# Row maxima of a fused attention and MLP layer, turned by VectorE's 32x32 transposition instead of by products

## The chip, the cores and the metric

One core of a Trainium2 chip runs the whole program. The metric is the device time of one execution in microseconds (us), as the median of several executions. The engines are named as the profile names them: PE is TensorE's matmul unit and PEld its weight load, DVE is VectorE, ACT is ScalarE, POOL is GpSimd, SP is SyncE, which here issues every DMA. SBUF is the on-chip working memory, PSUM the accumulators, in eight banks of 128 partitions by 512 float32.

## The reference

The input is `x` of 2048 rows by 512 columns, float32. The layer adds three things: the input itself, an attention block, and an MLP with tanh-GELU, both of these on the normalised rows:

```python
xn = _layernorm(x, axis=-1)
return x + _A_ref(xn, A_wqkv, A_wo) + _B_ref(xn, B_w1, B_b1, B_w2, B_b2)

# _A_ref: 32 heads of 16 columns
scores = jnp.einsum("bhqd,bhkd->bhqk", q, k) * (Dh ** -0.5)
p = _softmax(scores, axis=-1)
o = jnp.einsum("bhqk,bhkd->bhqd", p, v)

# _B_ref: 512 -> 1792 -> 512
h = _gelu(jnp.einsum("bsd,df->bsf", x, w1) + b1)
return jnp.einsum("bsf,fd->bsd", h, w2) + b2
```

The softmax subtracts each row's maximum over all 2048 keys before the exponential, so every head needs the maximum of each of its 2048 score rows first.

## The kernel before, in words

Operands of the products are split into a high and a low float16 part, so that float16 products give nearly float32 results.

**Attention** goes through the scores twice. In the *S pass* PE computes a 128 query x 512 key tile of scores into a PSUM bank `pS`, and DVE reduces it to a column of maxima (line 259, `mt<-pS`). In the *E pass* PE computes the transposed scores (keys on partitions, queries on columns) into a bank `pT`, with the negated maximum added by two more rows of the contraction, and ACT takes the exponential (line 304, `pe<-pT`). PE then multiplies by the values (`pV`). The maxima therefore have to come from the S pass, where they are a column per query tile, into rows of the operand `qst` (rows 62, 63, 126 and 127), where the E pass reads them.

The work is cut into 32 **blocks** (8 groups of four heads x 4 blocks of 512 queries), a block into 16 **units**, and a unit into two **half-units**. A unit holds four S tiles and four E tiles of the block that lies 20 units behind (`LEAD = 20`). In each half-unit PE does two S and two E tiles, then value products of an earlier unit together with a number of **dense** products (`pD`): projections, the MLP and so on, taken from a stream of `Group`s.

The order of the instructions on each engine is written out by the program itself: `unit` emits the tiles, `tick` at the end of each unit runs what `later(n, fn)` has put off by n units, and `pooled` hands work to POOL in portions. Nothing reorders the result.

**The end of a block (the place of the change).** `s_end` (line 262) runs after the last unit of a block's S pass. DVE reduces the 64 collected columns to 16 columns of negated maxima, one per head and query tile, in `mneg`, 128 x 32 with the last 16 columns zero (line 270). `store` is put off by one unit. In it, a bank `pt` is taken out of the same rotation of three banks from which the S tiles take theirs (`banks("S")`); two products with the identity (line 277), each over 64 partitions, turn `mneg` into 2 x 32 rows of 64; DVE writes these as a high and a low float16 part (`mhl`, lines 280 and 281); SP stores both to the DRAM tensor `m_d` in two transfers (line 284) and then loads them into the rows of `qst` in four (line 289), the first two for one pair of heads, the next two for the other.

Since the S tiles use three banks in turn, a tile can start on PE when the reduction of the tile three turns before has ended on DVE; the bank `pt` counts as a turn.

**The tanh of the GELU** is an ACT instruction (line 983) that `gelu` puts into the stream when POOL has prepared its input. Before, it was put off once, by a unit, when at most 8 products were left on the two sides of the current dense group, or no group was open.

Of the kernel before, what the change touches and what calls it, by code (L numbers as in the profile page):

```python
# [8 lines left out]
F32 = mybir.dt.float32  # L9
# [8 lines left out]
P = 128  # L18
# [30 lines left out]
def layer_kernel(ctx: ExitStack, tc: tile.TileContext, x, wqkv, wo, w1, b1, w2, b2, out):  # L49
# [163 lines left out]
    def later(n, fn, local=False):  # L213
        queue.append((slot[0] + n, fn, local))
# [47 lines left out]
    def s_end(u):  # L262

        t, i = divmod(u, 16)
        if i < 15:
            return
        g, qb = divmod(t, NQB)
        qs = qst[g % 2]
        mneg = mnegs[t % 2]
        nc.vector.tensor_reduce(mneg[:, :16], mt_of[t].rearrange("p h t k -> p (h t) k"), axis=AX.X, op=ALU.max, negate=True)  # L270
        given("dve", 220)

        def store():

            pt = banks("S")
            for a in range(2):
                nc.tensor.matmul(pt[32 * a:32 * a + 32, :64], mneg[64 * a:64 * a + 64, :],
                                 ident[64 * a:64 * a + 64, 64 * a:64 * a + 64], start=True, stop=True)
            mhl = work.tile([64, 2, 64], F16, name="mhl", bufs=2)
            nc.vector.tensor_scalar_mul(mhl[:, 0], pt[:64, :64], 1.0 / MROW)  # L280
            nc.vector.scalar_tensor_tensor(mhl[:, 1], pt[:64, :64], 1.0 / MROW, mhl[:, 0], op0=ALU.mult, op1=ALU.subtract)
            given("dve", 300)
            for a in range(2):
                nc.sync.dma_start(m_d[t, :, :, 64 * a:64 * a + 64], mhl[32 * a:32 * a + 16])
            for p in range(2):
                for a in range(2):
                    h = 2 * p + a
                    dst = qs[p][qb][64 * a + 62:64 * a + 64, :].rearrange("r (t q) -> r t q", q=P)
                    nc.sync.dma_start(dst, m_d[t, 4 * h:4 * h + 4].rearrange("t r q -> r t q"))

        later(1, store)
# [678 lines left out]
    def mlp():  # L970
# [5 lines left out]
        def gelu(hh, g, b, f):  # L976
            t1 = m2.tile([P, QB], F32, name="t1", bufs=2)

            def tanh(again=1):
                if again and (cur[0] is None or cur[0].left(0) + cur[0].left(1) <= 8):  # L980
                    later(1, lambda: tanh(0), True)
                    return
                nc.scalar.activation(t1, t1, AF.Tanh, scale=GELU_C * GELU_A)
                given("act", 600)
                later(1, rest, True)
# [217 lines left out]
```

## Time and profile before

| | us |
|---|---|
| median of 3 runs (1508.39 to 1509.23) | 1509.2 |
| the profiled execution | 1510.58 |
| its span, first to last instruction | 1508.8 |
| PE busy | 1474.4 |
| DVE busy | 1378.3 |
| ACT busy | 1233.8 |
| POOL busy | 716.5 |
| mean granted TensorE clock, as a share | 0.993 |

The busy time of PE is modelled and counts products that run side by side in quarters of the array once; DVE's instructions overlap their neighbours by some tens of nanoseconds. So neither number says alone which engine is waited for: that is read from the order of starts around a place. In the timeline view a line is a run of instructions of one kind on one engine: its start, its length from first start to last end, the engine, the source line, the operation, what is written and read, the shapes, and how many. Idle time of the engine just before stands in brackets with what ended it.

The kernel's first 130 us (normalisation, first projections) and its last 90 us (no S tiles any more) are stages of their own. Between them blocks follow each other some 41 us apart: `mneg` starts at 1168.14 and at 1209.25 us, for instance.

### The profile page before, as it was taken

The page shows a single profiled execution, that of the slowest core. Times are in us where ns is not written, and L with a number is a line of the kernel's source. Part 1 is how long each engine was busy: PE and PEld are TensorE (multiplying, and loading weights), DVE is VectorE, ACT ScalarE, POOL GpSimd, SP SyncE. Part 2 cuts the span into 40 slices and gives each one's busy share as a digit, 9 for nine tenths or more (in the row PEclk, how much of TensorE's full clock was granted, in tenths as well). Part 3 has the DMA queues.
Part 4 walks back from the last instruction along what each step waited for, and adds up shares of the span by engine and source line. Part 5 has one row for each costly group of instructions (what it writes and reads, how often), then busy time and mean ns, then how long its engine had stood idle before and what let it go on. Part 6 is the DMA issues. An engine that isn't in the chain of part 4 may idle for free.

```text
span 1508.8 us, 87920 instructions
## 1 busy us (share of the span) xinstructions
PE 1474.4 (98%) x39971; PEld 908.1 (60%) x39971; DVE 1378.3 (91%) x2372; ACT 1233.8 (82%) x2326; POOL 716.5 (47%) x750
## 2 busy tenths in 40 slices
PE   8998999999999999999999999999999999999997
PEld 4434556656666666666666666666666666666563
DVE  7898999999999999999999999999999999999612
ACT  5315878899999889999898998998999999988771
POOL 4113598547665545537544554665264465511000
PEclk9999999999999999999999999999999999999998
DMA  6454576633211311121112211121112111022412
GB/s 201 133 172 128 169 217 220 207 102 95 71 37 44 89 42 37 36 78 44 36 50 63 59 36 37 35 83 57 37 42 63 51 33 33 23 68 76 155 37 88
DMA packets 113677, 123.82 MB, mean 82 GB/s; under 512 B 24988, under 2 KB 85276, under 8 KB 113304
## 3 DMA queue, kind: packets, MB, share of 16 engines
q1 hardware_dynamic: 113304, 118.21, 25.6%
q8 instruction: 312, 5.11, 1.4%
q14 instruction: 61, 0.50, 0.1%
HBM read 80.61 MB, written 37.34 MB: 78 GB/s over the span
## 4 chain that ended last, share of the span: by engine, by line
PE 81%; DVE 15%; issue 2%; DMA 1%; ACT 0%; POOL 0%; SPq 0%; ACTq 0%; POOLq 0%
PE pV L170 21%; PE pD L170 20%; PE pS L170 19%; PE pT L170 15%; DVE mt L259 13%; PE pT L441 1%; PE pS L441 1%; DVE amx L675 1%; PE pT L540 1%; PE pD L441 1%; PE pV L540 0%; DVE mneg L270 0%; DMA wch<-in_B_w_dram 0%; DMA xs<-in_A_x_dram 0%; DVE bs L709 0%
## 5 line engine op out<-in xcount | busy, mean ns | idle before, releaser
L259 DVE TENSOR_REDUCE mt<-pS 128x1 f32<-128x512 f32 x2048 | 1278.7, 682 | 40.5 <-PE pS L170 23.5
L304 ACT ACTIVATE pe<-pT 128x512 f32<-128x512 f32 x2048 | 1099.6, 601 | 144.8 <-PE pS L170 62.3
L170 PE MATMUL pV<-pe,vv 64*32 64x512 f32 x8192 | 1088.8, 598 | 1.5 <-issue 1.5
L170 PE MATMUL pT<-qst,kst 64*32 64x512 f16 x8192 | 669.7, 377 | 3.3 <-DMA qst<-m_d 1.4
L170 PE MATMUL pS<-kst,qst 62*32 62x512 f16 x8192 | 637.9, 378 | 9.6 <-DVE mt L259 6.2
L170 PE MATMUL pD<-xb,wc 64*32 64x512 f16 x5376 | 371.8, 375 | 0.0
L170 PE MATMUL pD<-w_s,g 64*32 64x512 f16 (+1 forms) x6144 | 361.8, 348 | 0.0
L170 PEld LDWEIGHTS <-kst 64*32 64x32 f16 x8192 | 254.0, 92 | 129.1 <-issue 49.7
L170 PEld LDWEIGHTS <-qst 62*32 62x32 f16 x8192 | 246.9, 92 | 138.6 <-issue 64.1
L170 PEld LDWEIGHTS <-g 64*32 64x32 f16 x6144 | 195.3, 92 | 84.6 <-issue 0.8
L170 PEld LDWEIGHTS <-wc 64*32 64x32 f16 x5376 | 177.4, 92 | 95.5
L170 PEld LDWEIGHTS pV<-pe,vv 64*32 64x32 f32 x8192 | 176.9, 105 | 5.5 <-issue 2.2
L1018 POOL TENSOR_SCALAR hh<-hh,fac,b_s 128x512 f32<-128x512 f32 x56 | 43.0, 768 | 271.5 <-ACT hh L1016 271.5
L170 PE MATMUL pD<-xt,wqk_h 64*32 64x512 f16 x1920 | 128.6, 375 | 3.1 <-issue 3.1
L360 POOL TENSOR_TENSOR osb<-osb,rb 128x512 f32<-128x512 f32 x31 | 39.8, 1283 | 138.4 <-DMA rb<-den_d 130.2
L1045 POOL TENSOR_TENSOR xa<-xa,yt 128x512 f32<-128x512 f32 x32 | 41.0, 1281 | 111.2 <-ACT yt L1043 111.2
L170 PEld LDWEIGHTS <-wqk_h 64*32 64x32 f16 x1920 | 59.5, 92 | 32.5 <-issue 5.8
L1082 DVE SCALAR_TENSOR_TENSOR ac<-pS,gs,ac 128x512 f32<-128x512 f32 x20 | 15.0, 751 | 65.2 <-PE pS L170 55.5
L996 POOL TENSOR_TENSOR t<-t,hh 128x512 f32<-128x512 f32 x56 | 71.8, 1282 | 4.7
L989 POOL TENSOR_TENSOR t<-t,hh 128x512 f32<-128x512 f32 x56 | 71.8, 1282 | 4.7
L991 POOL TENSOR_TENSOR g<-t,g 128x512 f16<-128x512 f32 x56 | 65.2, 1165 | 4.7
L170 PE MATMUL pS<-wo_s,oc 64*32 64x512 f16 x1008 | 61.0, 377 | 0.4
(140 smaller groups left out, 928.3 us busy)
## 6 DMA issues: line engine op xcount, KB each, us to landing
wch<-in_B_w_dram SPq DMA_DIRECT2D x28, 512.0 KB
wc<-w_d SPq DMA_DIRECT2D x56, 256.0 KB
qk_d<-stg SPq DMA_DIRECT2D x32, 256.0 KB
rb<-den_d SPq DMA_DIRECT2D x124, 64.0 KB
w_d<-wsp SPq DMA_DIRECT2D x28, 256.0 KB
kst<-qk_d SPq DMA_DIRECT2D x128, 48.0 KB
qst<-qk_d SPq DMA_DIRECT2D x128, 48.0 KB
xs<-in_A_x_dram SPq DMA_DIRECT2D x16, 256.0 KB
```

The lines of the kernel that those rows point to most:

```text
L170: p = nc.tensor.matmul(*args, **kw)
L259: nc.vector.reduce_max(mt_of[t][:, n, qt, kb:kb + 1], s, axis=AX.X)
L304: nc.scalar.activation(pe, st, AF.Exp, scale=factor(exp_scale, sexp[0:1, g // 2:g // 2 + 1]))
L360: pooled((1280, lambda: nc.gpsimd.tensor_tensor(osb, osb, rb, op=ALU.mult)), (620, lambda: nc.gpsimd.tensor_scalar(ot[:, 0], osb, 1.0, 0.0 ...
L441: nc.tensor.matmul(self.bank, lhs, rhs, start=start, stop=self.last and self.over())
L540: nc.tensor.matmul(pj, xt[:, i, c, t * P:(t + 1) * P], wh[j][:, c, :], start=(n == 0), stop=(n == 11))
L675: nc.vector.tensor_reduce(dst, v, axis=AX.XY if len(v.shape) == 3 else AX.X, op=ALU.max, apply_absolute_value=True)
L989: (1280, lambda: nc.gpsimd.tensor_tensor(t1, t1, hh, op=ALU.mult)),
L991: (1160, lambda: nc.gpsimd.tensor_tensor(g[:, 1, f, :], t1, g[:, 0, f, :], op=ALU.subtract)),
L996: (1280, lambda: nc.gpsimd.tensor_tensor(t1, t1, hh, op=ALU.mult)),
L1018: later(1, lambda: pooled((690, lambda: nc.gpsimd.tensor_scalar(hh, hh, scale, bias, op0=ALU.mult, op1=ALU.add)), (0, lambda: gelu(hh, g, ...
L1045: add = lambda: nc.gpsimd.tensor_tensor(xa, xa, yt, op=ALU.add)
```

## The change

In `store`, the two products and the bank go. DVE's own transposition turns each 32 x 32 square of `mneg` by itself, SBUF to SBUF, so that partitions 32a to 32a+15 of `mrow` hold the maxima of queries 32a to 32a+31. The two instructions that split into float16 parts now read `mrow` in SBUF (128 x 32) in place of the bank (64 x 64), and the rows of 128 queries go to DRAM in four transfers of 32 columns in place of two of 64. In `gelu`, the tanh is put off while 4 or fewer products are left (before: 8), and up to twice.

```diff
         def store():
 
-            pt = banks("S")
-            for a in range(2):
-                nc.tensor.matmul(pt[32 * a:32 * a + 32, :64], mneg[64 * a:64 * a + 64, :],
-                                 ident[64 * a:64 * a + 64, 64 * a:64 * a + 64], start=True, stop=True)
-            mhl = work.tile([64, 2, 64], F16, name="mhl", bufs=2)
-            nc.vector.tensor_scalar_mul(mhl[:, 0], pt[:64, :64], 1.0 / MROW)
-            nc.vector.scalar_tensor_tensor(mhl[:, 1], pt[:64, :64], 1.0 / MROW, mhl[:, 0], op0=ALU.mult, op1=ALU.subtract)
+            pt = work.tile([P, 32], F32, name="mrow", bufs=2)
+            nc.vector.transpose(pt, mneg)
+            mhl = work.tile([P, 2, 32], F16, name="mhl", bufs=2)
+            nc.vector.tensor_scalar_mul(mhl[:, 0], pt, 1.0 / MROW)
+            nc.vector.scalar_tensor_tensor(mhl[:, 1], pt, 1.0 / MROW, mhl[:, 0], op0=ALU.mult, op1=ALU.subtract)
             given("dve", 300)
-            for a in range(2):
-                nc.sync.dma_start(m_d[t, :, :, 64 * a:64 * a + 64], mhl[32 * a:32 * a + 16])
+            for a in range(4):
+                nc.sync.dma_start(m_d[t, :, :, 32 * a:32 * a + 32], mhl[32 * a:32 * a + 16])
...
-            def tanh(again=1):
-                if again and (cur[0] is None or cur[0].left(0) + cur[0].left(1) <= 8):
-                    later(1, lambda: tanh(0), True)
+            def tanh(again=2):
+                if again and (cur[0] is None or cur[0].left(0) + cur[0].left(1) <= 4):
+                    later(1, lambda: tanh(again - 1), True)
                     return
```

The new program is two lines shorter, so that a line behind `store` has a number lower by two. On PE nothing but the products with the identity disappears; here is PE at the end of block 26 (`wc` is a dense operand, `kst` and `qst` those of the scores), before:

```order
51716 L170 LDWEIGHTS wc
51717 L170 MATMUL pD<-xb,wc 32x512
51718 L277 MATMUL pS<-ident,mneg_118 32x64 x2
51719 L170 LDWEIGHTS qst_0_3_100
51720 L170 MATMUL pS<-kst_0_1_82,qst_0_3_100 32x512
```

and now:

```order
51688 L170 LDWEIGHTS wc
51689 L170 MATMUL pD<-xb,wc 32x512
51690 L170 LDWEIGHTS wc
51691 L170 MATMUL pD<-xb,wc 32x512
51692 L170 LDWEIGHTS qst_0_3_100
51693 L170 MATMUL pS<-kst_0_1_82,qst_0_3_100 32x512
```

The first S tile of the next unit follows the dense products at once. DVE at the same place, between the reductions of the S tiles, before:

```order
371 L259 TENSOR_REDUCE mt<-pS 128x1 x16
372 L270 TENSOR_REDUCE mneg_118<-mt 128x16
373 L259 TENSOR_REDUCE mt<-pS 128x1 x4
374 L280 TENSOR_SCALAR mhl<-pS 64x64
375 L281 SCALAR_TENSOR_TENSOR mhl<-pS,mhl 64x64
376 L259 TENSOR_REDUCE mt<-pS 128x1 x44
```

and now:

```order
397 L259 TENSOR_REDUCE mt<-pS 128x1 x16
398 L270 TENSOR_REDUCE mneg_118<-mt 128x16
399 L259 TENSOR_REDUCE mt<-pS 128x1 x4
400 L276 STREAM_TRANSPOSE mrow<-mneg_118 128x32
401 L278 TENSOR_SCALAR mhl<-mrow 128x32
402 L279 SCALAR_TENSOR_TENSOR mhl<-mrow,mhl 128x32
403 L259 TENSOR_REDUCE mt<-pS 128x1 x44
```

There is one instruction more between the fourth and the fifth reduction of the new block, and the two that stood there read SBUF alone.

The order of ACT changes at a single place of the program, some 367 us into it, where `hh<-pD` empties the bank of a finished dense group, before:

```order
137 L304 ACTIVATE pe<-pT 128x512 x14
138 L1016 ACTIVATE hh<-pD 128x512
139 L983 ACTIVATE t_9374<-t_9374 128x512
140 L304 ACTIVATE pe<-pT 128x512 x4
141 L983 ACTIVATE t_9644<-t_9644 128x512
```

and now:

```order
137 L302 ACTIVATE pe<-pT 128x512 x10
138 L981 ACTIVATE t_9380<-t_9380 128x512
139 L302 ACTIVATE pe<-pT 128x512 x4
140 L1014 ACTIVATE hh<-pD 128x512
141 L302 ACTIVATE pe<-pT 128x512 x4
142 L981 ACTIVATE t_9650<-t_9650 128x512
```

The tanh stands four exponentials earlier, no longer next to the emptying of the bank; POOL's two portions that follow from these two change places accordingly.

## The prediction

> **What bounds the kernel now.** I read the page's chain of waits first, then the windows of 40 us (span, PE, PEld, DVE, ACT, POOL busy, clock, DMA share, GB/s), and then, because neither decides it, the timeline around the end of one block.
>
> ```profile
> PE 81%; DVE 15%; issue 2%; DMA 1%; ACT 0%; POOL 0%; SPq 0%; ACTq 0%; POOLq 0%
> 1200.00:1240.00 40.00, 39.88 (x1163) 24.91 (x1154) 39.08 (x66) 36.46 (x70) 21.68 (x23) 1.00 0.14 41
> ```
>
> PE and DVE are both nearly full (39.88 and 39.08 of 40 us), and the granted clock is 1.00. PE carries the chain, but 15% of it runs over DVE. The timeline of DVE says where:
>
> ```profile
> 1209.25 0.22 DVE L270 TENSOR_REDUCE mneg<-mt 128x16 f32<-128x64 f32 x1
> 1209.39 2.47 DVE L259 TENSOR_REDUCE mt<-pS 128x1 f32<-128x512 f32 x4
> 1211.78 0.20 DVE L280 TENSOR_SCALAR mhl<-pS 64x64 f16<-64x64 f32 x1
> 1212.02 0.22 DVE L281 SCALAR_TENSOR_TENSOR mhl<-pS,mhl 64x64 f16<-64x64 f32 x1
> 1212.16 5.05 DVE L259 TENSOR_REDUCE mt<-pS 128x1 f32<-128x512 f32 x8
> ```
>
> Four reductions in a row take 2.39 us from start to start (1209.39 to 1211.78), 0.60 each: that is DVE at its own pace. Now the same moment on PE, each line chosen for its start:
>
> ```profile
> 1208.61 0.40 PE L170 MATMUL pT<-qst,kst 64*32 64x512 f16 x4
> ...
> 1208.78 0.45 PE L170 MATMUL pS<-kst,qst 62*32 62x512 f16 x8
> ...
> 1209.87 0.40 PE L170 MATMUL pS<-kst,qst 62*32 62x512 f16 x4
> ...
> 1210.26 0.40 PE L170 MATMUL pS<-kst,qst 62*32 62x512 f16 x4
> ...
> 1211.15 0.38 PE L277 MATMUL pS<-ident,mneg 64*32 64x64 f32 x3
> 1211.32 0.10 PEld L170 LDWEIGHTS <-qst 62*32 62x32 f16 x3
> ...
> 1211.91 0.10 PEld L170 LDWEIGHTS <-qst 62*32 62x32 f16 x3 [0.46 <-issue]
> ...
> 1212.80 0.39 PE L170 MATMUL pS<-kst,qst 62*32 62x512 f16 x4
> ```
>
> Half-units begin at 1208.61, 1209.87 and 1211.15 (here with the products with the identity), 1.26 and 1.28 apart, and the next one 1.65 later. I take 1.25 for an undisturbed half-unit (the pause ahead of the products is a part of the 1.28) and 2.51 for a unit; DVE, at its own pace, needs 2.39: in a steady unit PE sets the time and DVE waits 0.12. At a block's end DVE gets 0.14 of `mneg` (to 1209.39) and 0.38 of `mhl` (1211.78 to 1212.16) on top, and PE stands still between 1211.32 and 1211.91: the second S tile waits for a bank. Because `pt` took a turn of the three banks, that tile needs the bank whose reduction is the fourth of the new block, begun at 1211.18 and ended at 1211.86. The half-unit loses 1.65 - 1.25 = 0.40 us: 0.17 to the products with the identity (1211.15 to 1211.32), 0.23 to the bank. Without the wait the second tile would have started some 0.2 behind 1211.32, as at 1208.78 behind 1208.61 (both S tiles in one line), so it waited 0.39: a wait costs about 0.6 of its length, the rest the half-unit wins back. Other boundaries look like this one; there are 31 with S tiles behind them, so boundaries cost 12.4 us, the most that the change can win there.
>
> **The boundary, part by part.** On PE the products and the turn of the bank go; both waits above go with them. On DVE one instruction more stands before the fifth reduction. Its cost is not in the trace; the nearest rows:
>
> ```profile
> L259 DVE TENSOR_REDUCE mt<-pS 128x1 f32<-128x512 f32 x2048 | 1278.7, 682 | 40.5 <-PE pS L170 23.5
> L270 DVE TENSOR_REDUCE mneg<-mt 128x16 f32<-128x64 f32 x32 | 7.0, 219 | 1.0
> L717 DVE TENSOR_SCALAR sd<-mv 128x4 f32<-128x4 f32 x4 | 0.7, 170 | 0.0
> L724 DVE SCALAR_TENSOR_TENSOR sd<-sd 128x4 f32<-128x4 f32 x4 | 0.6, 158 | 0.1
> L348 DVE RECIPROCAL dn<-dn 64x32 f32<-64x32 f32 x31 | 10.3, 334 | 0.0
> ```
>
> A transposition of 32 columns reads 32 and writes 32: no less than a small instruction (0.16), no more than the slow reciprocal of 32 columns (0.33). I take 0.22, as for `mneg`, which moves a like number of elements. The two float16 instructions on 32 columns: 0.17, and 0.16 + 0.03 = 0.19 (28 more columns at 1.03 ns, since 512 columns take 0.68 and 64 take 0.22). Each waits for the one ahead, which adds 0.035 (0.20 long, 0.24 apart at 1211.78), and the last overlaps the next reduction by 0.08 (0.22 long, 0.14 apart). Sum 0.255 + 0.205 + 0.11 = 0.57 us against 0.38.
>
> By the Trainium skill ("VectorE: DVE Perf Modes", The three transpose paths) a 128x128 transposition of 16-bit elements takes VectorE 311 ns. That length as an estimate would make the sum 0.66, and 2 us more over all boundaries; no run here shows one yet.
>
> What is late next? At 1211.78 DVE begins the three and ends them at 1212.35. The fifth reduction then ends 0.68 later, at 1213.03. Without a stall PE wants its bank for the fourth S tile of the unit at 1209.87 + 2.51 + 0.39 = 1212.77 (0.39 from 1209.87 to 1210.26): it waits 0.3 and loses 0.18. The second tile of the next unit wants the bank of the seventh reduction, which begins at 1213.55 and ends at 1214.23, at 1212.38 + 1.25 + 0.18 + 0.2 = 1214.01: it waits 0.22 and loses 0.14. Loss after: 0.32, so 0.08 is won per boundary, x 31 = **-2.5 us**. With 0.45 us for the three both waits shrink by 0.12 and it is 0.17 (-7.1 us), with 0.70 it is 0.48 (+2.5 us).
>
> **A wait that the change adds.** The two float16 instructions now read only SBUF, where POOL works, too. This trace has small DVE instructions of that kind during POOL's work:
>
> ```profile
> 138.31 0.69 DVE L480 TENSOR_TENSOR sexp<-fac 128x1 f32<-128x1 f32 x1
> 137.82 1.16 POOL L153 TENSOR_TENSOR wqk_h<-wq,wqk_h 128x512 f16<-128x512 f32 x1
> 185.97 0.98 DVE L480 TENSOR_TENSOR sexp<-fac 128x1 f32<-128x1 f32 x1
> 185.78 1.16 POOL L153 TENSOR_TENSOR wqk_h<-wq,wqk_h 128x512 f16<-128x512 f32 x1
> 178.79 0.28 DVE L139 TENSOR_SCALAR fac<-sc_c 128x2 int32<-128x2 int32 x1
> 176.91 2.14 POOL L905 TENSOR_TENSOR wsp<-wch,wsp 128x1024 f16<-128x1024 f32 x1
> ```
>
> With two inputs in SBUF (the first two) a 0.15 us instruction takes 0.69 and 0.98 and ends within 0.02 of POOL's; with one (the third) it takes 0.28 and does the same. `mhl`'s second part becomes the first kind, its first part the second. By the Trainium skill ("SBUF — State Buffer", Who interferes with whom) VectorE in a two-port mode, or with two inputs in SBUF, shares a port pair with GpSimd, and whichever is second waits for the other's whole instruction; the rows agree. So I laid POOL's timeline over the moments at which the two would ask. Two of them:
>
> ```profile
> 305.51 0.21 DVE L280 TENSOR_SCALAR mhl<-pS 64x64 f16<-64x64 f32 x1
> 305.44 1.27 POOL L360 TENSOR_TENSOR osb<-osb,rb 128x512 f32<-128x512 f32 x1
> 469.50 0.22 DVE L280 TENSOR_SCALAR mhl<-pS 64x64 f16<-64x64 f32 x1
> 469.78 1.28 POOL L989 TENSOR_TENSOR t<-t,hh 128x512 f32<-128x512 f32 x1
> ```
>
> At the first, the first part would ask at 305.76 and wait until 0.15 before 306.71: 0.8 us. At the second, POOL's instruction lines up while the first part works, and the second part waits for all of it, 0.95. Nine of the 31 moments are of the first sort (3.7 us together), three of the second (2.9). What DVE is late passes to PE at about 0.8: **+5.3 us**. Bounds: 0, if instructions this short slip past, and 10, if POOL stands less favourably.
>
> **The two further stores** lengthen the way of the maxima to the E pass:
>
> ```profile
> 965.06 1.21 SPq L284 DMA_DIRECT2D m_d<-mhl  x2
> 969.25 1.16 SPq L289 DMA_DIRECT2D qst<-m_d  x4
> 972.07 0.40 PE L170 MATMUL pT<-qst,kst 64*32 64x512 f16 x4
> 518.24 1.16 SPq L289 DMA_DIRECT2D qst<-m_d  x4
> 520.02 0.43 PE L170 MATMUL pT<-qst,kst 64*32 64x512 f16 x8 [1.45 <-DMA qst<-m_d]
> ```
>
> Two stores cost SP 1.2 us, so two more cost 1.2. At 520.02 PE did wait, 1.78 after the first load was issued; at 965.06 the first load has 972.07 - 1.78 - 969.25 = 1.04 us to spare, and there the landing took 3 us. Where it lands quickly there is more. So the 1.2 us is mostly hidden in that reserve. Where the reserve is used up it costs PE the excess, as at 520.02: **+1 us** for the few such blocks, bounds 0 and 6.
>
> **The tanh.**
>
> ```profile
> 364.69 2.22 ACT L304 ACTIVATE pe<-pT 128x512 f32<-128x512 f32 x4 [0.29 <-PE pS L170]
> 367.03 0.60 ACT L1016 ACTIVATE hh<-pD 128x512 f32<-128x512 f32 x1
> 367.52 0.62 ACT L983 ACTIVATE t<-t 128x512 f32<-128x512 f32 x1
> 368.07 0.40 PE L170 MATMUL pS<-kst,qst 62*32 62x512 f16 x4
> 368.68 0.40 PE L170 MATMUL pT<-qst,kst 64*32 64x512 f16 x4 [0.20 <-ACT pe L304]
> ```
>
> ACT has 0.29 us free per unit, `hh` and tanh together take 1.0, and PE's `pT` stands 0.6 behind `pS`. With the tanh a unit earlier ACT catches up between the two: **-0.4 us**, bounds -0.6 and 0.
>
> **The sum** against the profiled execution's 1510.6 (span 1508.8 and 1.8 around it): -2.5 + 5.3 + 1 - 0.4 = +3.4, 1514.0. The median of the runs is 1.4 below the profiled one, so I forecast **1512.6 us**.
>
> **The rivals.** (1) *The bank sets PE free.* The wait behind the block's end is short enough for PE to win it back: the boundary loses 0.17 in place of 0.40 (-7.1 us), and POOL's waits, partly hidden in the same way, cost a third: -7.1 + 1.8 - 0.4 + 1 = -4.7, 1504.5. For it: 0.16 of 0.39 was won back at 1211.91. Against it: DVE has more to do than before, and it is DVE that is late. It decides below 0.45 us for the three. (2) *Nothing that can be told.* If the short instructions pass POOL, -2.5 - 0.4 + 1 = -2, 1507 to 1510. For it: POOL is busy only 21.68 of 40 us. Against it: the 0.69 and 0.98 above. (3) *The loads of `qst` come to lie on the path.* If at some twelve boundaries the 1.2 us comes on top of a late landing and exceeds the reserve by 0.4: +5 more, 1518. Against it: a landing that waits for other traffic is not made longer by two small stores.
>
> **How the numbers follow.** My forecast has 0.42, rival 1 0.20, rival 2 0.28, rival 3 0.10. A measurement of this kernel tells some 0.2% (3 us) from no change. Faster by more: 0.17 of rival 1 and 0.06 of rival 2, 0.23. Within: 0.03 of rival 1, 0.22 of rival 2 and 0.10 of the forecast, whose 3.4 lies near the bound, 0.35. Slower: 0.32 of the forecast and rival 3, 0.42. The likeliest case alone is 1510 to 1517; the range is 1503 to 1521, from rival 1 to the upper ends of POOL's and the loads' terms.
>
> **What would show it.** In the changed profile: the half-unit behind a block's end at 1.25 us on PE, and the one behind it at 1.45 to 1.6; STREAM_TRANSPOSE at 0.2 us; the two `mhl` rows mostly at 0.17 and 0.19, but in a third of the blocks up to 1.2, ending with a POOL instruction; `pT` waiting for `qst<-m_d` in few blocks; no 0.6 us gap at 368. The forecast is wrong if the `mhl` rows never grow, or if PE does not wait in the half-unit after.

## The result, and the profile after

| | before | after |
|---|---|---|
| median of the runs | 1508.4 us (11 runs) | 1516.3 us (11 runs) |
| ratio, 95% interval | | 1.0054 (1.004 to 1.0069) |
| profiled execution, its span | 1510.6, 1508.8 | 1516.8, 1514.9 |

The change costs 0.54%, 8 us. The forecast was slower by 3.4 us, 1512.6; the measured time lies inside the range, and closer to the third rival's 1518 than to 1512.6. The sign and three of the four terms hold up in the trace. The fourth, the two further stores, was set at +1 us and is the one that failed. One execution of the kernel of experiment 3 below took 2978 us, twice the others; it counts in the median given there and not in the ratio.

The page of the changed kernel, in the chain of waits and the groups of PE:

```profile
PE 65%; DVE 21%; DMA 5%; POOL 3%; issue 2%; SPq 2%; ACT 0%; DVEq 0%; POOLq 0%; ACTq 0%
...
L170 PE MATMUL pT<-qst,kst 64*32 64x512 f16 x8192 | 674.4, 378 | 9.1 <-DMA qst<-m_d 5.1
L170 PE MATMUL pS<-kst,qst 62*32 62x512 f16 x8192 | 628.0, 379 | 14.5 <-DVE mt L259 12.6
```

The same two groups in the page before:

```profile
L170 PE MATMUL pT<-qst,kst 64*32 64x512 f16 x8192 | 669.7, 377 | 3.3 <-DMA qst<-m_d 1.4
L170 PE MATMUL pS<-kst,qst 62*32 62x512 f16 x8192 | 637.9, 378 | 9.6 <-DVE mt L259 6.2
```

Both waits of PE grew: the S tiles wait 14.5 us in place of 9.6, mostly for VectorE, and the E products (`pT`) wait 9.1 in place of 3.3, of which 5.1 in place of 1.4 for the maxima (`qst<-m_d`). The chain, which had 1% of DMA, has 5% now, and SP's queue, which had 0%, has 2%.

The three instructions at a block's end, all 32 blocks (minimum, median and maximum in ns):

```profile
L276 DVE STREAM_TRANSPOSE mrow<-mneg x32: 201/204/214, 113.2 to 1426.5; 128x32 f32<-128x32 f32 x32
L278 DVE TENSOR_SCALAR mhl<-mrow x32: 181/182/1044, 113.4 to 1426.8; 128x32 f16<-128x32 f32 x32
L279 DVE SCALAR_TENSOR_TENSOR mhl<-mrow,mhl x32: 191/192/1158, 113.6 to 1427.2; 128x32 f16<-128x32 f32 x32
```

The forecast had 0.22, 0.17 and 0.19 us. The transposition never waits; the two float16 instructions, otherwise 0.18 and 0.19, go up to 1.04 and 1.16.

An undisturbed block end, the same one as in the prediction, first VectorE and then PE:

```profile
1218.87 0.20 DVE L276 STREAM_TRANSPOSE mrow<-mneg 128x32 f32<-128x32 f32 x1
1219.11 0.18 DVE L278 TENSOR_SCALAR mhl<-mrow 128x32 f16<-128x32 f32 x1
1219.33 0.19 DVE L279 SCALAR_TENSOR_TENSOR mhl<-mrow,mhl 128x32 f16<-128x32 f32 x1
1219.44 1.88 DVE L259 TENSOR_REDUCE mt<-pS 128x1 f32<-128x512 f32 x3
```

```profile
1218.21 0.40 PE L170 MATMUL pT<-qst,kst 64*32 64x512 f16 x4
...
1219.47 0.40 PE L170 MATMUL pS<-kst,qst 62*32 62x512 f16 x4
...
1220.17 0.40 PE L170 MATMUL pS<-kst,qst 62*32 62x512 f16 x4 [0.15 <-DVE mt L259]
...
1221.04 0.40 PE L170 MATMUL pT<-qst,kst 64*32 64x512 f16 x4
...
1222.36 0.39 PE L170 MATMUL pS<-kst,qst 62*32 62x512 f16 x4
```

The three take 0.57 us (1218.87 to 1219.44), as forecast. Half-units begin at 1218.21, 1219.47 and 1221.04: 1.26 and then 1.57 apart, where the forecast had 1.25 and "1.45 to 1.6". The loss against 1.25 is 0.01 + 0.32 = 0.33 us (forecast 0.32, before 0.40); the half-unit behind these takes 1.32 (to 1222.36), another 0.07.

A block end at which POOL stands in the way, VectorE and POOL:

```profile
472.35 0.18 DVE L278 TENSOR_SCALAR mhl<-mrow 128x32 f16<-128x32 f32 x1
472.57 1.15 DVE L279 SCALAR_TENSOR_TENSOR mhl<-mrow,mhl 128x32 f16<-128x32 f32 x1
473.64 1.87 DVE L259 TENSOR_REDUCE mt<-pS 128x1 f32<-128x512 f32 x3
```

```profile
472.39 1.28 POOL L987 TENSOR_TENSOR t<-t,hh 128x512 f32<-128x512 f32 x1
```

POOL's instruction begins while the first of the two works, and the second ends 0.05 behind it (473.72 and 473.67): this is the second kind of wait of the prediction. Over the trace nine waits of the first kind add up to 4.0 us and three of the second to 2.8; the forecast had nine with 3.7 and three with 2.9. All twelve end 0.04 to 0.05 us behind an instruction of POOL.

**Where the time went, place by place.** The order of the S tiles is the same in both kernels, so I took the start of each unit's third S tile as its mark in both traces and compared the distances from mark to mark. Units are counted from 0 behind the end of a block's S pass: in units 0 and 1 PE meets the boundary, in 3 and 4 the block's E pass begins. Outside the places named, almost every unit behind the ends of blocks 4 to 29 agrees within 0.01 us. What lies ahead of these and behind them differs from one execution to the next by -8.6 to +10 us in all the traces below, of whatever kernel, so the mechanisms are read from blocks 4 to 29. In us against the trace of the kernel before:

| trace | span | units 0 and 1, behind the block ends | units 3 and 4, where an E pass begins | unit 12 | other units | outside blocks 4 to 29 |
|---|---|---|---|---|---|---|
| after | +6.1 | +3.3 | +4.4 | -0.1 | -1.7 | +0.2 |

The +3.3 is the boundary (-0.09 x 26 = -2.4) and POOL's waits (+5.7). The +4.4 are waits for the maxima; the others hold the tanh with -0.6 (unit 9 behind block 5), and a further -0.7 in one unit where the trace of the kernel before had a delay of its own.

### The profile page after: what moved, and what is told of

Its sections match the earlier page's. It is cut to its first block, busy times and chain, and to the rows that moved or that the text cites. A ratio compares the mean times of both kernels' runs of the same rounds, so it can differ in the third digit from the quotient of the medians.

```text
span 1514.9 us, 87759 instructions
## 1 busy us (share of the span) xinstructions
PE 1472.6 (97%) x39843; PEld 903.0 (60%) x39843; DVE 1384.1 (91%) x2404; ACT 1234.2 (81%) x2326; POOL 716.9 (47%) x750
## 4 chain that ended last, share of the span: by engine, by line
PE 65%; DVE 21%; DMA 5%; POOL 3%; issue 2%; SPq 2%; ACT 0%; DVEq 0%; POOLq 0%; ACTq 0%
DVE mt L259 18%; PE pV L170 17%; PE pS L170 16%; PE pD L170 16%; PE pT L170 12%; DMA m_d<-mhl 1%; PE pS L439 1%; PE pT L439 1%; DMA w_d<-wsp 1%; DMA wch<-in_B_w_dram 1%; POOL wsp L903 1%; DMA qk_d<-stg 1%; DMA ac<-acc_d 1%; DVE amx L673 1%; DVE mhl L278 1%
## 5 line engine op out<-in xcount | busy, mean ns | idle before, releaser
L170 PE MATMUL pS<-kst,qst 62*32 62x512 f16 x8192 | 628.0, 379 | 14.5 <-DVE mt L259 12.6
```

What stands on the lines that cost most here:

```text
L170: p = nc.tensor.matmul(*args, **kw)
```

## The experiments

Ratios are to the kernel before, run on the same chip beside it. Where two changed kernels are compared, it is by these ratios.

### 1. Four stores in the kernel before

```
-            for a in range(2):
-                nc.sync.dma_start(m_d[t, :, :, 64 * a:64 * a + 64], mhl[32 * a:32 * a + 16])
+            for a in range(4):
+                nc.sync.dma_start(m_d[t, :, :, 32 * a:32 * a + 32], mhl[32 * (a // 2):32 * (a // 2) + 16, :, 32 * (a % 2):32 * (a % 2) + 32])
```

> The kernel before (products with the identity, the scores' bank, two float16 instructions out of PSUM), but the maxima are stored by four transfers of 32 columns in place of two of 64: the same pieces and the same count as in the changed kernel. The whole computation stays. Theory A (the stores are the term that was set too small: +1 in the prediction, and about +3 to +6 in the trace of the changed kernel): 1511.5 to 1514.5 us against 1508.4, and pT's idle time in the page's group rises from 3.3 us to 6 or more, with qst<-m_d as what ended it; the first load is issued 3.7 us or later behind mhl's end, where it now is 2.4. Theory B (the size in the prediction was right, and what the changed kernel's trace shows there is an accident of what else stood in SP's queue): 1509 to 1510 us, pT's idle time under 5.

Measured: 1516.9 us against 1510.9, ratio 1.0039 (1.002 to 1.0057), which is 6 us (3 to 8.6) for the stores alone. The page of this kernel:

```profile
L170 PE MATMUL pT<-qst,kst 64*32 64x512 f16 x8192 | 667.2, 378 | 10.0 <-DMA qst<-m_d 5.5
```

pT's idle time is 10.0 us (3.3 before). The two units behind the block ends are as before (0.0), the E passes' first units cost +4.8. So theory A holds: the stores by themselves, with nothing changed in what VectorE and PE do, cost 6 of the 8 us that the whole change costs. The term of +1 was wrong by a factor of several.

### 2. The high part alone

```
-                nc.sync.dma_start(m_d[t, :, :, 32 * a:32 * a + 32], mhl[32 * a:32 * a + 16])
+                nc.sync.dma_start(m_d[t, :, 0, 32 * a:32 * a + 32], mhl[32 * a:32 * a + 16, 0])
...
-                    dst = qs[p][qb][64 * a + 62:64 * a + 64, :].rearrange("r (t q) -> r t q", q=P)
-                    nc.sync.dma_start(dst, m_d[t, 4 * h:4 * h + 4].rearrange("t r q -> r t q"))
+                    dst = qs[p][qb][64 * a + 62:64 * a + 63, :].rearrange("r (t q) -> r t q", q=P)
+                    nc.sync.dma_start(dst, m_d[t, 4 * h:4 * h + 4, 0:1].rearrange("t r q -> r t q"))
```

> The changed kernel, but only the high float16 part of the maxima is stored and loaded (four stores of 16 pieces in place of 32, loads of one row in place of two); the low part is computed and left out, so the row that is subtracted is rounded to float16, the same in numerator and denominator. By the rows of the traces a store of 32 pieces takes SP 0.6 us and a load of 8 pieces 0.3, so I estimate 0.39 for a store of 16 and 0.24 for a load of 4: the first load is issued 0.9 us earlier, and the last row is there 1.1 us earlier. Theory A (stores and loads cost the changed kernel 3 us or more): -2 to -4 us against it, 1512 to 1514.5, pT's idle time from 9.1 us down to 6 or less. Theory B (all of the loss is VectorE's, by POOL's waits): no change, 1515.5 to 1517, and pT's idle time falls without the span falling.

Measured: 1519.4 us, ratio 1.0062 (1.0039 to 1.0086): no gain over the changed kernel's 1.0054. Neither theory had this: the estimate of the loads, 0.24, was wrong. SP's issues in this kernel, ns:

```profile
L282 SPq DMA_DIRECT2D m_d<-mhl x128: 302/418/1567, 114.0 to 1439.6; - x128
L287 SPq DMA_DIRECT2D qst<-m_d x128: 551/563/656, 116.8 to 1443.0; - x128
```

and in the changed kernel:

```profile
L282 SPq DMA_DIRECT2D m_d<-mhl x128: 547/590/1985, 113.8 to 1432.5; - x128
L287 SPq DMA_DIRECT2D qst<-m_d x128: 224/257/463, 117.7 to 1435.4; - x128
```

The store of half the pieces takes 0.42 us in place of 0.59, as estimated (0.39), but the load of one row takes 0.56 where that of two rows took 0.26. What the stores give, 4 x 0.17, the loads take back, 4 x 0.31. The run doesn't tell the theories apart. It shows only that the waits for the maxima can be larger still (+13.9 us in blocks 4 to 29 of its trace) and that they then show in the time.

### 3. No wait for POOL

```
-            nc.vector.tensor_scalar_mul(mhl[:, 0], pt, 1.0 / MROW)
-            nc.vector.scalar_tensor_tensor(mhl[:, 1], pt, 1.0 / MROW, mhl[:, 0], op0=ALU.mult, op1=ALU.subtract)
+            nc.vector.tensor_reduce(mhl[:, 0], pt.unsqueeze(2), axis=AX.X, op=ALU.max)
+            nc.vector.tensor_reduce(mhl[:, 1], mhl[:, 0].unsqueeze(2), axis=AX.X, op=ALU.max)
```

with `MROW = 0.5`.

> The changed kernel, but its two float16 instructions on the turned maxima are two reductions over an axis of length one (128x32, one input, the kind that reads the 128x64 maxima in this kernel), which copy the maximum rounded to float16, and the row of ones holds 0.5: the low part of the maxima is replaced by a second copy of the high one. Theory A (the waits of the two for POOL, 3.96 and 2.86 us in the changed kernel's trace, pass to PE at about 0.8 to 1): -5 to -6.5 us against the changed kernel, 1510 to 1511.5; no mhl row over 0.3 us. Theory B (PE wins most of these waits back): -1 to -2.5, 1514 to 1515. Theory C (a reduction waits for POOL as well): no change, rows up to 1.2 us as before.

Measured: 1517.8 us, ratio 1.0049 (1.0029 to 1.0069): in the time no change, as theory C had it. The two rows, all 32 blocks:

```profile
L278 DVE TENSOR_REDUCE mhl<-mrow x32: 185/186/189, 115.5 to 1430.6; 128x32 f16<-128x32 f32 x32
L279 DVE TENSOR_REDUCE mhl<-mhl x32: 186/186/188, 115.7 to 1430.8; 128x32 f16<-128x32 f16 x32
```

But the mechanism of theory C falls: none of the 64 reductions waits, though 35 of them overlap an instruction of POOL. In the trace the two units behind the block ends go from +3.3 to -2.4, 5.7 us less, as theory A has it. The time, however, hardly moves, and in the trace the waits for the maxima rose from +4.4 to +9.4. Either the two are linked, or they are separate and this execution had bad luck. Experiments 7 and 9 to 12 bear on this.

### 4. The tanh alone, in the kernel before

```
-            def tanh(again=1):
-                if again and (cur[0] is None or cur[0].left(0) + cur[0].left(1) <= 8):
-                    later(1, lambda: tanh(0), True)
+            def tanh(again=2):
+                if again and (cur[0] is None or cur[0].left(0) + cur[0].left(1) <= 4):
+                    later(1, lambda: tanh(again - 1), True)
```

> The kernel before with the change's second edit alone (tanh put off twice while 4 products or fewer are left, in place of once while 8 are). Prediction: -0.4 us, which one time can't tell; in the trace tanh and hh of the third block lie in different units, and the pT 0.6 us behind pS at 368 us is at its usual distance of 0.4. Rival: the edit also moves other tanh and costs ACT's pe somewhere else, seen as new waits of pT for a bank or of pV for pe, +1 us or more in units elsewhere.

Measured: one execution, 1504.6 us, 0.2 below the lowest of the runs of the kernel before beside it (1504.8 to 1516.0), from which one time can't tell it. In the trace the unit concerned is 0.58 us shorter (forecast 0.4), and no unit behind it became longer on that account. ACT's two instructions there:

```profile
361.29 0.63 ACT L983 ACTIVATE t<-t 128x512 f32<-128x512 f32 x1
363.96 0.60 ACT L1016 ACTIVATE hh<-pD 128x512 f32<-128x512 f32 x1
```

They stand 2.67 us apart, about a unit, where they stood 0.49 apart before (367.03 and 367.52). The rival falls.

### What stands ahead of the stores

Block 13 of the changed kernel shows what SP does ahead of late stores. Its `mhl` ended at 680.46; first SP's queue and then PE:

```profile
674.25 4.61 SPq L401 DMA_DIRECT2D qst<-qk_d  x8
678.90 3.01 SPq L354 DMA_DIRECT2D rb<-den_d  x4
681.95 0.42 SPq L560 DMA_DIRECT2D wc<-w_d  x1
682.47 2.48 SPq L282 DMA_DIRECT2D m_d<-mhl  x4
687.26 1.16 SPq L287 DMA_DIRECT2D qst<-m_d  x4
```

```profile
688.90 0.43 PE L170 MATMUL pT<-qst,kst 64*32 64x512 f16 x8 [1.26 <-DMA qst<-m_d]
```

The first store is issued 2.0 us late, because the loads of the next head group's stacks (32 transfers in eight units, every fourth block) fill SP's queue right up to the block end. In the kernel before, the late block at 520 us has the same ahead of it:

```profile
507.23 1.83 SPq L403 DMA_DIRECT2D qst<-qk_d  x4
509.11 2.83 SPq L356 DMA_DIRECT2D rb<-den_d  x4
512.04 1.88 SPq L557 DMA_DIRECT2D xb<-xn_d  x3
514.02 1.90 SPq L284 DMA_DIRECT2D m_d<-mhl  x2
```

There `mhl` had ended at 511.05, and the stores came 2.97 later. How late the first store comes behind `mhl` in the blocks that load stacks (5, 9, 13, 17, 21, 25), in us:

| trace | 5 | 9 | 13 | 17 | 21 | 25 |
|---|---|---|---|---|---|---|
| before | 0.89 | 2.97 | 0.03 | 0.40 | 1.16 | 0.03 |
| after | 0.03 | 1.36 | 2.01 | 0.03 | 0.03 | 0.03 |
| four stores in before (1) | 2.04 | 2.01 | 0.90 | 0.62 | 1.69 | 0.03 |
| no wait for POOL (3) | 3.75 | 1.89 | 1.77 | 0.03 | 0.03 | 0.79 |
| tanh alone in before (4) | 0.86 | 1.81 | 0.68 | 0.92 | 1.81 | 2.35 |

It differs from trace to trace: single issues that mostly take 0.42 us sometimes take over 1 (13 of the 107 loads of `qst` from 200 us on in the changed kernel's trace, up to 1.67). With two stores a lateness up to 1.2 us costs nothing in these traces, 1.81 costs 0.65 and 2.97 costs 1.9; with four, the last store comes 1.3 us later still.

Late issue is only half of it. Against the kernel before with the stacks spread (experiment 11), in whose trace no E pass of blocks 4 to 29 waits for the maxima, the E passes of the changed kernel wait 6.3 us: 3.0 in blocks 9 and 13, whose stores were issued late, and 3.3 in blocks whose first store left at once. Block 18 is one of these, SP and then PE:

```profile
888.02 2.48 SPq L282 DMA_DIRECT2D m_d<-mhl  x4
893.71 1.35 SPq L287 DMA_DIRECT2D qst<-m_d  x4
```

```profile
895.56 0.43 PE L170 MATMUL pT<-qst,kst 64*32 64x512 f16 x8 [0.38 <-DMA qst<-m_d]
```

The stores are issued by 890.50, and the loads, which wait for them to land, come 3.2 us later, where 1.2 to 1.3 is usual. With two stores as slow a landing (3.0 us, at 965.06 in the prediction) left PE its reserve; with four the first load comes 1.3 us later, and PE waits. What makes single landings slow no run shows.

### 5 and 6. The stacks' loads later, in the changed kernel and in the one before

```
-        if g + 2 < NG and pos[0] - LEAD >= 64 * (g + 1) + 3:
+        if g + 2 < NG and pos[0] - LEAD >= 64 * (g + 1) + 14:
```

> The changed kernel, but the loads of the next head group's stacks (32 transfers, four per unit over eight units) begin 11 units later: in more_stacks the bound is 64 * (g + 1) + 14 in place of + 3. They then stand in SP's queue behind the stores and loads of the maxima of every fourth block (t = 5, 9, 13, ..., 25), not ahead of them. Theory A (the four stores cost time because SP's queue is late there: each of these blocks' first store was issued 1.2 to 4 us behind mhl in one trace or another, and 1.3 us more of stores exceed the reserve): first store at 0.1 us or less behind mhl in these blocks, pT's idle time from 9.1 us in the changed kernel's trace to 5 or less, and 3 to 6 us less than the changed kernel: a ratio to the kernel before of 1.001 to 1.003 in place of 1.0054. Theory B (it is the landing of the stores, not the queue): the waits stay, ratio 1.0045 to 1.006.

> The same bound (+ 14 in place of + 3) in the kernel before. Its trace has one such wait of any size in those blocks (1.45 us in a row of pT at 520 us), other traces of it with two stores had 0.5 to 1 us in two or three more. Theory A: -1 to -3 us, ratio 0.998 to 0.9995. Theory B (loads of the stacks later collide with something else): no gain, ratio 0.9995 to 1.002.

Measured: the changed kernel 1534.1 us, ratio 1.0163 (1.0142 to 1.0184); the kernel before 1509.6, ratio 1.0006 (0.9989 to 1.0024). The first store now comes 0.03 us behind `mhl` in all six blocks, and the waits for the maxima in blocks 4 to 29 fall from +4.4 to +1.1 and, in the kernel before, by 2.0. So far theory A of both; the times are not what it forecast. Unit 12 of every fourth block grew, by 13.2 us and by 2.6 in all: in the kernel before the gain is gone, which was its theory B, and in the changed kernel it is lost several times over. The trace of the latter is its fastest execution (1525.1); what the 9 us from there to its median are, no trace shows. VectorE, SP and PE at the first of these places in the changed kernel with the stacks later:

```profile
377.05 0.34 DVE L346 RECIPROCAL dn<-dn 64x32 f32<-64x32 f32 x1 [4.23 <-DMA dn<-den_d]
```

```profile
366.45 4.70 SPq L401 DMA_DIRECT2D qst<-qk_d  x8
...
371.81 2.50 SPq L365 DMA_DIRECT2D ot_d<-ot  x4
374.36 1.26 SPq L343 DMA_DIRECT2D dn<-den_d  x1
```

```profile
377.99 0.62 PE L170 MATMUL pS<-kst,qst 62*32 62x512 f16 x4 [3.95 <-DVE mt L259]
```

The same queue, another victim: the load of `dn`, from which the denominators' reciprocal is made, now stands behind the stacks. The reciprocal waits for it at the head of VectorE's queue, behind it the reductions, behind them the scores' banks, and PE. In blocks 4 to 29 of both kernels' own traces that wait does not exist. The stacks were only pushed from one deadline onto another.

### 7. Both edits

```
+            nc.vector.tensor_reduce(mhl[:, 0], pt.unsqueeze(2), axis=AX.X, op=ALU.max)
+            nc.vector.tensor_reduce(mhl[:, 1], mhl[:, 0].unsqueeze(2), axis=AX.X, op=ALU.max)
...
+        if g + 2 < NG and pos[0] - LEAD >= 64 * (g + 1) + 14:
```

> The two together: the changed kernel with the two reductions that copy the rounded maximum twice (row of ones 0.5, low part left out), and with the stacks' loads later. With the copies alone the trace showed no wait for POOL and 5.7 us less at the block ends of blocks 4 to 29, but 5 us more of waits for the maxima, and no less time in all. Theory A (the two are separate terms, and the larger wait there was one execution's and the median's scatter): 5 to 6 us less than with the stacks later alone, a ratio to the kernel before of 0.997 to 0.9995. Theory B (what POOL no longer delays is given back at the loads of the maxima, since SP's queue keeps its own pace): within 2 us of the kernel with the stacks later alone.

Measured: 1522.9 us, ratio 1.0088 (1.0068 to 1.0108), with unit 12 at +18.0 and the waits for the maxima at +0.1. Its ratio is far from theory A's 0.997 to 0.9995, because of unit 12. Against the same placing with POOL's waits, 1.0163, it is 11 us better (7 to 16), and in the traces the block ends differ by 8.0 (+5.5 and -2.5). Theory B falls: with most of the waits for the maxima out of the way, POOL's waits do count.

### 8. One float16 transposition

```
-            pt = work.tile([P, 32], F32, name="mrow", bufs=2)
-            nc.vector.transpose(pt, mneg)
-            mhl = work.tile([P, 2, 32], F16, name="mhl", bufs=2)
-            nc.vector.tensor_scalar_mul(mhl[:, 0], pt, 1.0 / MROW)
-            nc.vector.scalar_tensor_tensor(mhl[:, 1], pt, 1.0 / MROW, mhl[:, 0], op0=ALU.mult, op1=ALU.subtract)
+            mhl = work.tile([P, 32], F16, name="mhl", bufs=2)
+            nc.vector.transpose(mhl, mneg)
...
-                nc.sync.dma_start(m_d[t, :, :, 32 * a:32 * a + 32], mhl[32 * a:32 * a + 16])
+                nc.sync.dma_start(m_d[t, :, 0, 32 * a:32 * a + 32], mhl[32 * a:32 * a + 16])
             for p in range(2):
-                for a in range(2):
-                    h = 2 * p + a
-                    dst = qs[p][qb][64 * a + 62:64 * a + 64, :].rearrange("r (t q) -> r t q", q=P)
-                    nc.sync.dma_start(dst, m_d[t, 4 * h:4 * h + 4].rearrange("t r q -> r t q"))
+                dst = qs[p][qb][62::64, :].rearrange("r (t q) -> r t q", q=P)
+                nc.sync.dma_start(dst, m_d[t, 8 * p:8 * p + 8, 0].rearrange("(a t) q -> a t q", a=2))
```

with `mneg` in float16 and `MROW = 1.0`, the tanh as changed and the stacks later. The low part of the maxima is left out.

> A version that takes the changed kernel's idea without what made it dear: the block's negated maxima are reduced to float16 at once (128x16 float16; the row of ones is 1), one transposition of 128x32 float16 turns them, and nothing else of VectorE stands there; four stores of 16 pieces, and two loads of one row for two heads each in place of four; tanh as changed, the stacks' loads later. The low part of the maxima is left out, which rounds what is subtracted in numerator and denominator alike. By the working for the boundary, 0.25 us of VectorE in place of 0.57 leaves no wait for a bank: 0.3 us less per block end than the changed kernel and 0.4 less than before, 10 to 12 us over 27 to 31 block ends, 1 to 3 us for the stacks and 0.5 for tanh: ratio to the kernel before 0.989 to 0.993. Rival: the transposition of float16 waits for POOL's port (the float32 one, at 201 to 214 ns, never did): then up to 1.2 us in nine blocks, ratio 0.994 to 0.997.

Measured: 1508.9 us, ratio 0.9994 (0.998 to 1.0008), not the 0.989 to 0.993 expected. The block ends gave what the working had said (-10.4 us in blocks 4 to 29, 0.40 each), the waits for the maxima another -2.0, and unit 12 took 13.9 back, by the same `dn`. The rival falls, too: the float16 transposition took 202 to 213 ns throughout.

### 9 to 12. The stacks' loads spread

The stacks need a place where nothing on SP is due: behind the maxima's loads and ahead of the next block's sums there are four units. Half of the loads go there, half into the same place a block later.

```
-        if g + 2 < NG and pos[0] - LEAD >= 64 * (g + 1) + 3:
+        if g + 2 < NG and pos[0] - LEAD >= 64 * (g + 1) + 13 + k + 12 * (k > 3):
```

> The changed kernel, the stacks' loads in the units in which SP's queue has nothing due: half of them (four units of four transfers) from unit 13 behind an E block's start, behind the stores of the maxima, and half 16 units later, in place of eight units in a row. All eight in a row from unit 14 took the wait for the maxima away (blocks 4 to 29: from +4.4 to +1.1 us against before in the two units concerned), but made dn<-den_d late, for which VectorE's reciprocal then waited, and PE for it (+12 us in unit 12 of every fourth block). Theory A (SP's queue is what made the four stores dear): both waits are gone, pT's idle time 5 us or less, no unit 12 longer by over 0.5 us; left are POOL's waits (+5.7 in blocks 4 to 29), the boundary (-0.1 us each) and tanh (-0.6): about +2 us against before, ratio 1.000 to 1.0025. Theory B (the stores' landing costs time wherever the stacks stand): ratio 1.004 to 1.006 as in the changed kernel.

> The same with the two copies that don't wait for POOL (maxima rounded to float16 twice, low part left out, row of ones 0.5). Theory A (separate terms): 5 to 6 us less than the run beside it with the stacks spread alone, ratio to before 0.996 to 0.999. Theory B (given back elsewhere): within 2 us of it.

> The kernel before with the stacks' loads spread like that. Its own waits for the maxima at every fourth block are gone (2 us in its trace), unit 12 stays as it is: -1 to -3 us, ratio 0.998 to 0.9995. Rival: no gain, since its two stores always fit in the reserve: 0.9995 to 1.001.

> One float16 transposition in place of the three instructions (as before: maxima rounded to float16, low part left out, row of ones 1, four stores of 16 pieces, two loads for two heads each), with the stacks' loads spread. With the stacks in a row from unit 14 its block ends had 0.38 us less than before in each of 26 blocks (10.35 us) and the waits for the maxima 2 us less, but unit 12 of every fourth block 13 us more, and the time was that of before (ratio 0.9994). With the 13 us gone: ratio 0.989 to 0.993. If unit 12 keeps a third of them: 0.993 to 0.996.

Measured:

| kernel, stacks spread | median | ratio, 95% interval | profiled execution |
|---|---|---|---|
| changed | 1520.2 | 1.0064 (1.0043 to 1.0085) | 1510.1 |
| changed, no wait for POOL | 1510.6 | 0.9999 (0.9983 to 1.0015) | 1511.0 |
| before | 1506.5 | 0.998 (0.9967 to 0.9993) | 1506.5 |
| one float16 transposition | 1493.6 | 0.9897 (0.9877 to 0.9917) | 1489.2 |

By place, blocks 4 to 29, us against the trace of before (the float16 transposition with the stacks in a row beside them):

| trace | span | units 0 and 1 | units 3 and 4 | unit 12 | other units | outside |
|---|---|---|---|---|---|---|
| changed, spread | -0.6 | +4.8 | +0.9 | -0.1 | -0.8 | -5.5 |
| no wait for POOL, spread | +0.3 | -2.3 | +1.3 | -0.1 | -0.6 | +1.9 |
| before, spread | -4.1 | +0.1 | -2.0 | -0.1 | +0.7 | -2.9 |
| float16, in a row (8) | -3.1 | -10.4 | -2.0 | +13.9 | -0.9 | -3.8 |
| float16, spread | -21.4 | -10.5 | -2.0 | -0.1 | -0.3 | -8.6 |

The first store comes 0.03 us behind `mhl` in the six blocks of all four, and unit 12 is as before. The waits for the maxima are gone in the kernel before and in the version with one float16 transposition, but not in the two others, which still wait 2.9 and 3.3 us more than the kernel before with the same placing. Their first store is never late; the landing is. Block 12 of the changed kernel with the stacks spread, SP and then PE:

```profile
633.07 2.48 SPq L282 DMA_DIRECT2D m_d<-mhl  x4
638.81 1.16 SPq L287 DMA_DIRECT2D qst<-m_d  x4
```

```profile
640.49 0.43 PE L170 MATMUL pT<-qst,kst 64*32 64x512 f16 x8 [0.21 <-DMA qst<-m_d]
```

The loads come 3.3 us behind the last store here, and 2.7 in the same block of the kernel before with the stacks spread, where PE doesn't wait.

The kernel before and the float16 version came out as expected. The kernel before gains 3 us (1 to 5) by nothing but another place for the loads of the stacks. The version with one float16 transposition is 1.03% faster than the kernel before and beats both kernels of the case, with maxima rounded to float16. Its block end on VectorE:

```profile
1190.24 0.22 DVE L270 TENSOR_REDUCE mneg<-mt 128x16 f16<-128x64 f32 x1
1190.37 2.48 DVE L259 TENSOR_REDUCE mt<-pS 128x1 f32<-128x512 f32 x4
1192.76 0.20 DVE L276 STREAM_TRANSPOSE mhl<-mneg 128x32 f16<-128x32 f16 x1
1192.89 12.42 DVE L259 TENSOR_REDUCE mt<-pS 128x1 f32<-128x512 f32 x20
```

The fifth reduction starts 0.13 us behind the transposition, and VectorE then runs twenty of them on end.

The changed kernel with the stacks spread is the one that came out against its expectation: its ratio is nearest to theory B's, no better than the changed kernel's 1.0054. Its profiled execution (1510.1) is where theory A wanted it, with POOL's waits of 4.8 + 2.4 = 7.2 us in blocks 4 to 29 and the 2.9 at the slow landings, but the five other executions took 1514.9 to 1523.3. The kernel beside it, which differs only in that it doesn't wait for POOL, shows no such gap (1504.5 to 1513.4, profiled 1511.0). It is 10 us faster (6 to 14), more than the 5 to 6 expected, though its own ratio is above the 0.996 to 0.999 expected. So what the five have in addition comes with the two instructions that wait for POOL. The four traces with these two instructions have between 12 and 15 waits, which add up to 6.8, 8.7, 8.3 and 9.3 us: the sum depends on how POOL happens to stand. That it was larger still in those five executions would fit, but none of them has a trace, so it stays open.

Taken alone, then, neither cure makes the changed kernel faster: 1.0049 without POOL's waits and 1.0064 with the stacks spread, against 1.0054. The two together take away all of the 8 us (0.9999).

## Why the prediction came out as it did

**The bound and the boundary: right, the split by luck.** VectorE's lateness behind a block end sets the loss there, as forecast. The three instructions took 0.57 us, the loss 0.33 (forecast 0.32). Three lengths of VectorE's part now lie on one line of reasoning: 0.38 with a turn of the bank loses 0.40, 0.57 without it 0.31 to 0.33, and 0.13 next to nothing. The trace gives -2.4 us over 26 block ends (forecast -2.5 over 31). But the forecast made its 0.32 of two waits, each lost by 0.6 of its length: 0.18 for one of 0.3 (1213.03 - 1212.77 is 0.26) and 0.14 for one of 0.22. In the block shown the fourth S tile of the unit came 0.31 late (at 1220.17, 0.70 behind 1219.47, where 0.39 is usual) and the half-unit lost all of it, 0.32; the next lost 0.07. The factor 0.6 does not hold there, and the sum comes out because the second wait is smaller. The estimate by the page "VectorE: DVE Perf Modes" of the Trainium skill, 311 ns for a 128x128 transposition, was a bad guide for 32 columns: 204 ns measured, so the sum from rows was the better one. By the prediction's own factors that length would also have meant 3.3 us more over all boundaries, not 2.

**POOL's waits: right in the trace, in kind, number and size** (6.8 us of waits against 6.6 laid out). Their cost is somewhat higher than forecast: in blocks 4 to 29 the waits add up to 5.6 us and PE loses 5.7, all of it, where the term took 0.8. The rule of the Trainium skill ("SBUF — State Buffer", Who interferes with whom), that the second to ask waits for the other's whole instruction, agrees with all of them. In the time the term is 10 and 11 us with the stacks spread and with the stacks later (changed against no wait for POOL, each uncertain by 4 us), but under 1 with the stacks where they were (1.0054 against 1.0049, uncertain by as much). In the last case the trace of experiment 3 shows the waits for the maxima grown by 5 us. A PE that POOL holds up by a microsecond gives SP's queue that microsecond to catch up, so the two waits may cover each other; that is argued from one trace and from the times of the kernels with one cure and with both, not shown.

**The two further stores: the step that failed.** The prediction said: "the 1.2 us is mostly hidden in that reserve. Where the reserve is used up it costs PE the excess, as at 520.02: +1 us for the few such blocks". The mechanism is this one, the size is not: alone, the stores cost 6 us (3 to 8.6), the upper bound of the prediction. Two readings made the term small. First, the reserve of 1.04 us was read at 965.06, where the stores left at once and their landing took 3.0 us; two further stores take 1.3, so wherever a landing is as slow the reserve is exceeded. In the changed kernel the E pass also begins earlier behind the end of `mhl` (6.75 us in place of 7.04 in block 20). The prediction counted such blocks as hidden; in the trace after, the blocks with stores on time wait 3.3 us. Second, the wait at 520.02 was taken as one of a few, and what stood ahead of it in SP's queue was not used: the stores of that block came 2.97 us late, behind the stacks' loads, and the same stands ahead of every fourth block, in two more of which the stores were 0.9 and 1.2 late without harm yet. There part of the reserve was already spent before the change; in the trace after, the two late blocks wait 3.0 us. The third rival (loads on the path, 1518, chance 0.10) had the right place and the right mechanism for the first half. Its reason against, that a late landing isn't made longer by two stores, missed that the landing need not get longer: it begins 1.3 us later.

**The tanh: right** (-0.58 against -0.4).

**The sum.** -2.4 (boundary) + 5.7 (POOL) + 4.4 (maxima) - 1.7 (tanh and other units) + 0.2 (outside) = +6.2 between the traces (spans +6.1), against the forecast's +3.4. The difference is the stores' term, +4.4 against +1, less 1.3 in the other units, of which 0.7 is the delay that only the trace before had. Rival 1 (the bank sets PE free) falls with the 1.57 us at 1221.04, rival 2 (short instructions slip past POOL) with the rows of 1.04 and 1.16.

## What to carry to other kernels

A queue that is idle on average can be full at the moment that counts: before adding a transfer, read what stands ahead of it in its queue at each of its places, and when the first of its kind was really issued, not only how long one takes. If a transfer is moved, list what is due in the queue at the new place; here it only changed the victim until it was spread over free units. Read the landing at its slowest, too: a reserve smaller than what is added is no reserve in the blocks where it was measured. Small instructions that can wait for POOL are dear by what they wait for, so one float16 transposition that needs no second pass was worth more than the move out of the bank itself.

## What the runs showed of the hardware that I had not expected

**A long stall costs twice.** The windows of 1 us behind the stall of 3.95 us in the changed kernel with the stacks later (columns: span, PE, PEld, DVE, ACT, POOL busy, granted clock, DMA share, GB/s):

```profile
374.00:378.00 4.00, 0.05 (x7) 0.01 (x2) 0.95 (x3) 0.65 (x2) 1.15 (x1) 0.95 0.24 58
378.00:379.00 1.00, 1.00 (x20) 0.58 (x27) 1.00 (x2) 0.29 (x1) 0.00 (x0) 0.50 0.51 105
379.00:380.00 1.00, 1.00 (x24) 0.38 (x12) 0.72 (x2) 0.31 (x1) 0.00 (x0) 0.50 0.79 253
...
381.00:382.00 1.00, 1.00 (x44) 0.62 (x29) 1.00 (x2) 1.00 (x3) 0.73 (x1) 0.98 0.85 263
```

PE came back at half its clock for 3 us; the same group of products takes 0.62 us there and 0.40 elsewhere. That unit cost 5.7 us by a stall of 4. Between 140 and 1300 us of all the traces there are twelve stretches at half clock, each begun during a stall of PE or within 1 us behind it. These stalls measured 1.61, 1.87, 1.98, 2.37, 2.61, 2.92, 3.56, 3.62, 3.70, 3.95, 3.98 and 4.08 us; that of 1.87 is the changed kernel's own, at 221 us, right behind another of 1.06. No half clock followed stalls of 2.03, 2.25, 2.26, 2.54, 2.58 and 2.66. A stretch lasted 3.41 us, or twice that in three of the four cases with 3.70 us and more of stall. The Trainium skill ("TensorE: Matmul & The Clock Gate", Part 1: The HAM clock gate) puts the change at an idle window of about 3.4 us, and asks as much time of work before the full clock is back. The way back agrees in nine of the twelve (3.41 us); the way down came behind shorter stalls, too, and the length of the stall alone did not decide it.

**The number of rows in a load changes SP's time the wrong way.** Two rows of four pieces took 0.26 us to issue, one row of four pieces 0.56, and one row for each of two heads 0.54. A transfer with fewer pieces isn't always the cheaper one to issue.
